# Casts of queries and keys by a two-input VectorE instruction, with the opening of the kernel in another order

## The chip, the cores and the metric

The kernel runs on one core of one Trainium2 chip. The metric is the device time of one execution in microseconds (us); lower is better. A core has five engines that run side by side and wait for each other by semaphores: TensorE (PE, with its weight load PEld), VectorE (DVE), ScalarE (ACT), GpSimd (POOL) and SyncE (SP). Loads and stores are issued from the queues of SP, ACT and POOL.

## The reference

A chunked attention is followed by a two-layer network. Attention has 4 batches, 8 heads, 768 positions and a head dimension of 64. Each chunk of 32 queries sees 8 memory positions, 16 positions to the left, its own 32 and 8 to the right:

```python
k_full = np.concatenate([mem_k, k_ctx], axis=2)
v_full = np.concatenate([mem_v, v_ctx], axis=2)
scores = scale * np.matmul(q_c, k_full.transpose(0, 1, 3, 2))
a = np.exp(scores - np.max(scores, axis=-1, keepdims=True))
out[:, :, c_start:c_end] = np.matmul(a / (a.sum(-1, keepdims=True) + 1e-9), v_full)
```

Its output, as 3072 rows of 512, goes through the network (512 to 2048 and back):

```python
h = x @ w_in
s = np.sin(alpha * h)
g = h + s * s / (alpha + 1e-09)
return g @ w_out
```

Inputs and output are f32; the kernel multiplies in bf16.

## The kernel before, in words

The work is split by batch. Stage i (0 to 3) does the network of batch i, and between its matmuls the attention of batch i + 1. The attention of batch 0 has no network to hide behind: it is the front, stage -1, and the subject here.

The order of everything is written out by hand. `WORDS` has one string of words for each stage, and `Stage.run` issues the instructions of one word after the other. Each engine runs its instructions in that order, and an instruction starts when its engine is free and its inputs and its buffer are there. The words that matter in the front:

- `a<n><engine>` (`do_a`): cast of one tile `kq_f[n]` of two heads, 128x768, from f32 to bf16, into `k_bf` (n = 0 to 2) or `q_bf` (n = 4 to 6), on ACT or DVE. A pair of heads is called a head pair, 0 to 3. These f32 tiles are loaded on the SP queue (k) and the ACT queue (q) before the first word. Head pair 3 is loaded by GpSimd in bf16 at once (`dk068`, `dq068`, L191).
- `k<hp>`, `l<hp>` (`turn`, L312): 12 transposes on TensorE of the keys, or the queries, of a head pair; `K<hp><engine>`, `L<hp><engine>` (`put_k` L323, `put_q` L332): the copy of the result from PSUM into `kT` or `qT`.
- `s<hp><half>` (`u_scores`, L350 and L358): masked scores of one head pair and half of the sequence, and their exponential on ACT (L365). `v<hp><half>` (`u_values`, L377): the product with v, then on DVE the reciprocal of the sums (L386) and the product with it into `x_blk` (L387).
- `T<hp><half>` or `t<hp><half>` (`turned`, L399 and L402): four transposes of `x_blk` and a copy into `xT`, the input of the network, on ACT (T) or DVE (t).
- `V<b><h0><h1>` (`load_v`, L204 to L215): loads of v for heads h0 to h1 of batch b, issued by GpSimd. `I<a><b>` (L249): loads of `w_in`, also by GpSimd. For a batch 0 word like `V024` the heads are 2 and 3.
- `C<x>`: constants. `Cl` transposes alpha (L828) and copies it (L829); `Ck` casts the memory keys (L807), transposes them and puts them into `kT`; `Cm` makes the mask rows; `Cf` and `m0` put the memory values into `vw` (L822, L224); `Cp`, `Cz`, `Cv`, `Cs` are GpSimd's memsets.
- `y<n>` (L725) and `z<n>` (L719): filler matmuls of zeros into a free PSUM bank, 4 of 128 columns for each `y1`, one of 512 columns for each `z1`. Nothing reads their results.
- `We`, `Ws`: loads of ScalarE's table for the exponential or the sine.

PSUM has eight banks; `Banks` hands them out in the order of the words, so an instruction may wait until the earlier user of its bank has been copied out. The network of batch 0 then begins with L457, whose eight matmuls for a block of 128 columns of `w_in` need all of `xT`; its first w_in blocks come with `I02`, the next with `I27`.

Of the kernel before, what the change touches and what calls it, by code (L numbers as in the profile page):

```python
# [17 lines left out]
ALU = mybir.AluOpType  # L18
# [1 line left out]

WORDS = (
    (
# [4 lines left out]
    ),  # L27
    (
# [93 lines left out]
def kernel(  # L122
# [12 lines left out]
    nc = tc.nc  # L135
# [5 lines left out]
    HP = H // 2  # L141
# [175 lines left out]
    def copier(eng):  # L317
        return {"A": nc.scalar.copy, "V": nc.vector.tensor_copy, "P": nc.gpsimd.tensor_copy}[eng]
# [214 lines left out]
    kq = (k_bf, q_bf)  # L533
    todo = [(hp, half) for hp in range(HP) for half in range(2)]

    class Stage:
# [145 lines left out]

        def do_a(self, a):
            hp = int(a[0]) % HP
            dst = kq[int(a[0]) // HP]
            copier(a[1])(  # L686
                dst[:, 2 * hp:2 * hp + 2].rearrange("p h r d -> p h (r d)"), kq_f[int(a[0])][:]
            )

        def do_C(self, a):  # L690
            consts_of[a]()
# [50 lines left out]
    kq_f = [mlp.tile([P, 2, 6 * D], F32, name="kq_f", tag=t) for t in ("u", "s2") * 4]  # L742
# [146 lines left out]
```

## Time and profile before

| | us |
|---|---|
| three runs, median (lowest to highest) | 214.51 (214.29 to 214.54) |
| the profiled execution, its own time | 214.68 |
| span of that execution in the profile | 212.8 |
| TensorE busy in the span | 204.9 (96%) |
| VectorE, ScalarE, GpSimd busy | 139.9, 143.7, 100.9 |

The span runs from the first to the last recorded instruction of the execution; 1.88 us of the profiled time lie outside it. Rows of a timeline give start, length, engine, line, operation, output and input, and in brackets how long the engine was idle before and what released it. Rows of the DMA view give the queue that issued a load, its size and the time from issue to landing. Line numbers are those of the kernel before; in the changed kernel, lines from `do_a` on stand two further down, and ScalarE's casts four.

### The profile page before, as it was taken

Reading aid. Unit: us, or ns where it says so; the run is one execution under the profiler, and the core shown is the slowest. Engines: PE = TensorE matmul, PEld = TensorE weight load, DVE = VectorE, ACT = ScalarE, POOL = GpSimd, SP = SyncE. Lnnn points to the kernel's source line nnn. Section 1 sums busy time; section 2 is a strip of 40 time slices with the busy share of each in tenths; the row PEclk is TensorE's granted clock in tenths of the full one; section 3 lists DMA queues with packets and bytes.
Section 4 is the critical chain, followed back from the end, with each engine's and each line's share of the span. In section 5 each row is a group of like instructions: output and inputs, shape, how many; then the busy total and the mean of one; then the engine's idle time right before and its main releaser. Section 6 shows DMA issues by size and latency. Waiting matters only on the chain.

```text
span 212.8 us, 4568 instructions
## 1 busy us (share of the span) xinstructions
PE 204.9 (96%) x1772; PEld 118.1 (55%) x1772; DVE 139.9 (66%) x210; ACT 143.7 (68%) x229; POOL 100.9 (47%) x142
## 2 busy tenths in 40 slices
PE   7879999999999999999999999999999999999994
PEld 7456665565455556555455555554555555554453
DVE  4788788999452749976766649897247187865010
ACT  2579898978848469968837199887856189891110
POOL 8998605589697297109795048664000022200000
PEclk9999999999999999999999999999999999999999
DMA  5999999999999999999999259999944400000312
GB/s 156 332 158 139 212 207 204 205 139 183 131 160 155 176 114 129 121 144 146 146 152 183 74 125 125 137 157 133 134 104 107 137 0 0 3 2 0 148 52 99
DMA packets 95853, 27.82 MB, mean 131 GB/s; under 512 B 84808, under 2 KB 92376, under 8 KB 95832
## 3 DMA queue, kind: packets, MB, share of 16 engines
q0 software_dynamic: 69152, 13.64, 89.3%
q1 hardware_dynamic: 25720, 12.68, 29.6%
q10 hardware_dynamic: 960, 1.21, 1.7%
q8 instruction: 14, 0.23, 0.6%
q14 instruction: 7, 0.06, 0.1%
HBM read 29.66 MB, written 6.29 MB: 169 GB/s over the span
## 4 chain that ended last, share of the span: by engine, by line
PE 78%; DVE 8%; ACT 5%; DMA 4%; issue 3%; SPq 1%; DVEq 0%; ACTq 0%
PE ps L495 39%; PE ps L457 30%; DMA kq_f<-in_k_dram 4%; PE ps L447 3%; DVE gT L484 2%; PE ps L418 2%; DVE x_blk L387 2%; DVE s L480 2%; ACT s L477 2%; PE ps L399 1%; ACT pt L365 1%; PE ps L312 1%; ACT u L472 1%; DVE q_bf L686 1%; DVE rinv L386 0%
## 5 line engine op out<-in xcount | busy, mean ns | idle before, releaser
L495 PE MATMUL ps<-w_out_sb,gT 128*128 128x512 bf16 (+1 forms) x400 | 89.1, 371 | 0.0
L457 PE MATMUL ps<-xT,w_in_sb 128*128 128x384 bf16 x512 | 85.9, 326 | 0.6 <-DVE gT L484 0.4
L484 DVE SCALAR_TENSOR_TENSOR gT<-s,inv_alpha,ps 128x768 bf16<-128x768 f32 x64 | 63.1, 1012 | 12.3 <-ACT s L477 5.2
L457 PEld LDWEIGHTS <-w_in_sb 128*128 128x128 bf16 x512 | 49.7, 98 | 35.2 <-issue 2.0
L472 ACT ACTIVATE u<-ps,alpha_sb 128x768 f32<-128x768 f32 x64 | 56.6, 894 | 16.9 <-PE ps L457 14.4
L495 PEld LDWEIGHTS <-gT 128*128 128x128 bf16 x400 | 37.1, 98 | 37.1 <-DVE gT L484 0.2
L480 POOL TENSOR_TENSOR s<-u 128x768 f32<-128x768 f32 x11 | 17.2, 1568 | 67.2 <-ACT u L472 56.4
L432 ACT ACTIVATE pt<-ps,biasm 128x256 bf16<-128x256 f32 x72 | 27.1, 488 | 10.5 <-PE ps L418 10.5
L502 DVE COPY o_sb<-ps 128x512 f32<-128x512 f32 (+1 forms) x15 | 10.0, 669 | 27.6 <-PE ps L495 25.7
L480 DVE TENSOR_TENSOR s<-u 128x768 f32<-128x768 f32 x23 | 21.9, 953 | 7.6 <-ACT u L472 7.5
L477 ACT ACTIVATE s<-u 128x768 f32<-128x768 f32 x30 | 25.0, 841 | 0.5
L387 DVE TENSOR_TENSOR x_blk<-ps,rinv 96x512 bf16<-96x512 f32 x32 | 22.0, 687 | 1.1
L502 ACT COPY o_sb<-ps 128x512 f32<-128x512 f32 (+1 forms) x10 | 5.7, 572 | 22.0 <-PE ps L495 22.0
L208 POOL DMA_DIRECT2D vw<-in_v_dram x13 | 12.0, 926 | 6.3 <-PE ps L399 5.4
L386 DVE RECIPROCAL rinv<-ps 96x8 f32<-96x8 f32 x32 | 6.4, 199 | 13.1 <-PE ps L447 12.7
L215 POOL DMA_DIRECT2D vw<-in_v_dram x13 | 13.3, 1024 | 1.6 <-DMA vw<-in_v_dram 1.6
L274 POOL DMA_DIRECT2D kst<-in_k_dram x16 | 13.0, 815 | 1.8 <-DMA vw<-in_v_dram 1.2
L268 POOL DMA_DIRECT2D kst<-in_k_dram x16 | 11.1, 691 | 2.1 <-DMA kst<-in_k_dram 1.0
L281 POOL DMA_DIRECT2D q_bf<-in_q_dram x12 | 10.7, 911 | 0.0
L402 ACT COPY xT<-ps 128x384 bf16<-128x384 bf16 x10 | 5.0, 496 | 8.2 <-PE ps L399 8.2
L447 PEld LDWEIGHTS <-pt 128*128 128x128 bf16 x192 | 8.2, 97 | 4.2 <-ACT pt L432 0.3
L447 PE MATMUL ps<-vw,pt 128*128 128x65 bf16 x192 | 8.9, 193 | 0.0
(83 smaller groups left out, 140.7 us busy)
## 6 DMA issues: line engine op xcount, KB each, us to landing
out_dram<-o_sb SPq DMA_DIRECT2D x23, 256.0 KB, 2.2
q_bf<-in_q_dram POOLq DMA_DIRECT2D x12, 128.0 KB, 7.7
kq_f<-in_k_dram SPq DMA_DIRECT2D x3, 384.0 KB, 6.2
kq_f<-in_q_dram ACTq DMA_DIRECT2D x3, 384.0 KB, 7.9
w_in_sb<-in_moe_w_in_dram POOLq DMA_DIRECT2D x1, 1152.0 KB, 12.9
vw<-in_v_dram POOLq DMA_DIRECT2D x7, 128.0 KB, 7.7
vw<-in_v_dram POOLq DMA_DIRECT2D x8, 112.0 KB, 8.1
kst<-in_k_dram POOLq DMA_DIRECT2D x14, 64.0 KB, 5.5
```

The lines of the kernel that those rows point to most:

```text
L215: nc.gpsimd.dma_start(vw[72:128, c0:hi, 0:D], win(vflat, base + QW * c0 + 48, hi - c0, 56))
L274: nc.gpsimd.dma_start(kst[72:72 + n, j, :].rearrange("p (h d) -> p h d", d=D), k[b, :, QW * j + 48:QW * j + 48 + n, :].rearrange("h p d -> ...
L387: nc.vector.tensor_tensor(out=x_blk[:].rearrange("p g e d -> p e g d"), in0=otv[0:QW, :, :, 0:D], in1=rinv[:].unsqueeze(3).to_broadcast([Q ...
L432: nc.scalar.activation(pt[:, 0:H * QW].rearrange("p (g e c) -> p g e c", g=2, e=4)[:, :, :, 32 * m:32 * m + 32], sc[:, :, 0:4 * QW].rearra ...
L447: nc.tensor.matmul(otv[:, e, hp, :], pt[:, QW * i:QW * i + P], vws[b % 2][:, 2 * hp + e, j, 0:D + 1],)
L457: nc.tensor.matmul(t["hT"][:, hf, 0:HALF], w_in_sb[:, kt, P * t["ft"]:P * t["ft"] + P], t["xT"][:, kt, HALF * hf:HALF * hf + HALF], start= ...
L472: nc.scalar.activation(t["u"][:], t["hT"][:, :, 0:HALF], ACTF.Sin, scale=alpha_sb[:, ft:ft + 1])
L477: nc.scalar.activation(s2[:], u[:], ACTF.Square)
L480: e.tensor_tensor(out=s2[:], in0=u[:], in1=u[:], op=ALU.mult)
L484: nc.vector.scalar_tensor_tensor(out=gT[:, ft, :].rearrange("p (e c) -> p e c", e=2), in0=t["s2"][:], scalar=inv_alpha[:, ft:ft + 1], in1= ...
L495: nc.tensor.matmul(o[:, c0:c1], gT[:, ft, P * s:P * s + P], w_out_sb[:, ft, c0:c1], start=(ft == 0), stop=(ft == FT - 1),)
L502: copier(state["engines"][state["o"] % len(state["engines"])])(o_sb[:, c0:c1], o[:, c0:c1])
```

## The change

VectorE's casts of `kq_f` tiles are no longer copies with a change of type: the same output is written as the larger of the tile and itself, which is the tile, by a two-input instruction. ScalarE's casts stay copies. The string of the front is written in another order. Beside the order it has fewer fillers (`y` 48 matmuls of 128 columns to 16, `z` 14 of 512 columns to 9), two `kT` copies change from ScalarE to VectorE (K1, K3), and three `xT` copies stand on VectorE instead of four. The loads of v's heads 2 and 3 (`V024`) stand ahead of `dk068` and `dq068` on GpSimd's queue, and the cast `a5V` stands ahead of `a2V`. The strings of the other stages are unchanged.

```diff
-        'y1 y1 y1 Ci y1 a4A We y1 Cb a1A y1 y2 y1 y1 dq068 Cl y1 Cm y1 Cf z1 z1 eVA z1 eVA a0A Ck m0 Cz z1 '
-        'dk068 Cp V024 z1 z1 V002 z1 a2V V068 z1 z1 Cv l0 z1 a5V z1 L0A k1 k0 z1 k2 l1 K1A V046 K0A a6V L1A '
-        's00 s10 s11 K2V l2 k3 L2V K3A s01 v11 dm l3 L3A v10 s20 v01 s30 v00 s31 v30 s21 v31 z1 T01 v20 T30 '
-        'I02 Cs T00 v21 t10 T20 t31 z1 t11 I27 t21 Ws '
+        'a4A We Cb Ci eVA a1A y1 Cl V024 Ck Cm Cp Cf z1 m0 z1 y1 z1 Cz dk068 eVA dq068 z1 z1 V002 a5V l0 a2V '
+        'a0A L0A k1 k0 K0A K1V V068 y1 y1 l1 k2 a6V L1A s00 Cv s10 s11 l2 K2V s01 k3 L2V V046 v10 dm K3V l3 '
+        'L3A v11 s30 v00 s31 v01 s20 s21 v30 Cs v31 T10 t01 v20 T00 z1 T11 v21 I02 z1 I27 z1 T31 T30 Ws t20 '
+        'z1 t21 '
...
         def do_a(self, a):
             hp = int(a[0]) % HP
-            dst = kq[int(a[0]) // HP]
-            copier(a[1])(
-                dst[:, 2 * hp:2 * hp + 2].rearrange("p h r d -> p h (r d)"), kq_f[int(a[0])][:]
-            )
+            dst = kq[int(a[0]) // HP][:, 2 * hp:2 * hp + 2].rearrange("p h r d -> p h (r d)")
+            src = kq_f[int(a[0])][:]
+            if a[1] == "V":
+                nc.vector.tensor_tensor(out=dst, in0=src, in1=src, op=ALU.max)
+            else:
+                copier(a[1])(dst, src)
```

## The prediction

> **What bounds the kernel now.** I read the page first, then a table of busy time by stretch, then the chain that ended last.
>
> ```profile
> span 212.8 us, 4568 instructions
> PE 204.9 (96%) x1772; PEld 118.1 (55%) x1772; DVE 139.9 (66%) x210; ACT 143.7 (68%) x229; POOL 100.9 (47%) x142
> 12.30:24.80 12.50, 10.36 (x229) 8.03 (x228) 11.29 (x22) 10.60 (x17) 10.98 (x17) 1.00 2.42 161
> 24.80:186.00 161.20, 160.63 (x1307) 90.07 (x1304) 113.08 (x154) 119.88 (x196) 78.58 (x90) 1.00 1.32 132
> ```
>
> The columns of the two stretches are length, then busy time of PE, PEld, DVE, ACT and POOL. From 24.8 us on TensorE is busy for 160.63 of 161.20 us: there is nothing to win there, and whatever moves the start of that stretch moves the end by as much. The change touches only what comes before, so I ask one question: when does the first matmul with w_in (L457) start?
>
> ```profile
> 2.57 8.45 DMA kq_f<-in_k_dram
> ...
> 11.05 0.56 DVE k_bf L686
> 11.61 1.68 DVE q_bf L686
> ...
> 13.33 0.55 PE ps L312 x12
> ...
> 14.60 2.22 ACT pt L365 x3
> ...
> 24.95 2.62 PE ps L457 x16
> ```
>
> The chain of waits (start, length, what) goes through the last load of k (head pair 2, down at 11.02), then two VectorE casts, then transposes, exponentials and the normalisation. VectorE's own timeline shows the whole stretch:
>
> ```profile
> 5.90 0.17 DVE L829 COPY alpha_sb<-ps 128x16 f32<-128x16 f32 x1 [2.31 <-PE ps L828]
> 9.36 1.22 DVE L224 COPY vw<-memv_st 8x4096 bf16<-8x4096 bf16 x1
> 11.05 0.56 DVE L686 CAST k_bf<-kq_f 128x768 bf16<-128x768 f32 x1 [0.47 <-DMA kq_f<-in_k_dram]
> 11.52 3.15 DVE L686 CAST q_bf<-kq_f 128x768 bf16<-128x768 f32 x2
> 14.60 0.94 DVE L323 COPY kT<-ps 128x768 bf16<-128x768 bf16 x1
> 16.10 0.96 DVE L332 COPY qT<-ps 128x768 bf16<-128x768 bf16 x1 [0.56 <-PE ps L312]
> 17.41 0.20 DVE L386 RECIPROCAL rinv<-ps 96x8 f32<-96x8 f32 x1 [0.35 <-PE ps L377]
> ...
> 23.70 0.69 DVE L387 TENSOR_TENSOR x_blk<-ps,rinv 96x512 bf16<-96x512 f32 x1
> 24.31 1.14 DVE L402 COPY xT<-ps 128x384 bf16<-128x384 bf16 x4
> ```
>
> The eight pairs of reciprocal and x_blk run almost without a gap from 17.41 to 24.39 (23.70 + 0.69), 6.98 us. So the end of the front is VectorE's queue counted from 11.02: casts, two PSUM copies, eight pairs.
>
> **The constants and the filler matmuls.** VectorE stood idle for 2.31 us until 5.90 because the transpose of alpha was queued behind 40 zero matmuls on TensorE. The new order has four of them ahead of it. The constants that follow end at 10.58 now (9.36 + 1.22); 2.31 earlier is 8.3. The order of the constants among themselves changes too, but their instructions are the same, so their sum stays. Their one unknown is when mem_k lands; it was there when its cast ran, and a late landing is in the range. That VectorE is free at 8.3 matters for the next step.
>
> **The casts.** The order is now a5V (q, pair 1), a2V (k, pair 2), a6V (q, pair 2); before, a5V stood behind a2V.
>
> ```profile
> 2.12 0.49 ACTq L748 DMA_DIRECT2D kq_f<-in_q_dram  x1
> kq_f<-in_q_dram ACTq DMA_DIRECT2D x1, 384.0 KB, 7.0
> 39.34 1.03 POOL L215 DMA_DIRECT2D vw<-in_v_dram  x1
> 39.83 0.95 DVE L480 TENSOR_TENSOR s<-u 128x768 f32<-128x768 f32 x1
> ```
>
> q's pair 1 was down at 2.12 + 7.0 = 9.1 and waited for k's pair 2 until 11.02. Moved ahead, its cast fits between 9.1 and 11.02 and leaves the path: 1.68 us gone. The two others become two-input instructions. No row shows a larger-of from f32 to bf16; the nearest is L480, a two-input instruction of one tile with itself, 128x768 f32, 0.95 us, and that one ran beside a load issue on GpSimd (39.34 to 40.37). The bounds are 0.56 (the k cast) and 1.68 (the q cast). I take 0.95. Ends overlap by about 0.09 (11.05 + 0.56 is 11.61, and the next starts at 11.52), so one step of 0.95 costs 0.86.
>
> The q cast was three times as long as the k cast with the same shape; GpSimd issues loads of v all through this time, and in the quoted row the two-input form showed no such stretch. The Trainium skill, SBUF — State Buffer, section "SBUF: two separate sides", says that VectorE and GpSimd share a port pair as an exclusive lock, and that an instruction with two SBUF inputs contends for it only against a GpSimd operation that reads SBUF. By that rule a cast costs 0.95 here even beside load issues, which the 39.83 row agrees with; the sum by it is the one below.
>
> **VectorE's queue after 11.02.** After the change it holds a2V, K1V (a kT copy that ScalarE had), a6V, K2V and L2V: five steps of 0.94 to 0.96, 0.86 each, 4.3 us, so the first reciprocal comes at about 15.4 instead of 17.41. That is 2.0 us. Back goes: K3V, another kT copy taken from ScalarE, +0.86 among the pairs, and one xT copy that now stands ahead of the last pairs (1.14 / 4 = 0.28). Eight pairs at 6.98: 15.4 + 6.98 + 0.86 + 0.28 = 23.5 against 24.39, a gain of 0.9. ScalarE loses two copies and gets one xT copy more; it was busy 10.60 of the 12.50 us, so this costs nothing.
>
> **The loads.** The new order moves the first v load (heads 2 to 3) ahead of q's and k's pair 3 on GpSimd's queue; w_in stays last.
>
> ```profile
> 3.66 0.94 POOL L191 DMA_DIRECT2D q_bf<-in_q_dram  x1
> q_bf<-in_q_dram POOLq DMA_DIRECT2D x1, 192.0 KB, 7.8
> 6.91 0.89 POOL L215 DMA_DIRECT2D vw<-in_v_dram  x1
> 12.03 0.87 POOL L215 DMA_DIRECT2D vw<-in_v_dram  x1
> vw<-in_v_dram POOLq DMA_DIRECT2D x1, 112.0 KB, 7.5
> 17.64 1.51 POOL L249 DMA_DIRECT2D w_in_sb<-in_moe_w_in_dram  x2
> w_in_sb<-in_moe_w_in_dram POOLq DMA_DIRECT2D x1, 640.0 KB, 8.1
> 21.94 0.42 PE L377 MATMUL ps<-vw,pt 128*128 128x65 bf16 x8
> q0 software_dynamic: 54, 0.04, 26.4%
> q0 software_dynamic: 1251, 0.15, 237.1%
> ```
>
> The last two rows (packets, MB, share of the 16 DMA engines) are GpSimd's DMA queue from 8 to 9 us and from 12 to 13: by 9 hardly anything of it had moved although its first load was issued at 3.66, and then it ran full of small packets. So its loads come down some 7.5 to 8 us after issue, in order, and the same bytes are through at the same time in either order. The two pieces of the first v load now take 3.66 to about 5.4, small memsets follow to about 6.3, k's pair 3 is issued then and q's pair 3 at about 7.0, as late as the second v piece before (6.91). It lands at 7.0 + 7.8 = 14.8; its transpose comes at about 15.2 (the queue above, before K3V). Cover 0.4 us. The v load of heads 6 to 7 lands at 12.03 + 7.5 = 19.5 as before. Behind it stand four value products with their pairs: 0.42 for the product, 4 x 6.98 / 8 = 3.5, the xT copy 0.28: 23.7. That is a little later than VectorE's own 23.5, so the loads set the end: 24.39 - 23.7 = 0.7. At the very end fewer VectorE copies of xT are left behind the last pair (two instead of four), worth about 0.1. Sum: **0.8 us earlier**. The larger w_in load is down at 17.64 + 8.1 = 25.7; its first user comes 2.62 us after the first L457, at 24.95 - 0.8 + 2.62 = 26.8, so this gain is covered; it would stop one above 1.8.
>
> The profiled execution took 214.68 (212.8 span and 1.88 around it), so it would take 213.9; it lies 0.17 above the median of the runs shown, 214.51. **Forecast for the median: 213.7.**
>
> **The rivals.**
>
> *The clock of TensorE comes up late (slower).* The row of granted clock says 1.00 throughout, yet matmul rates differ:
>
> ```profile
> 1.20 4.45 PE L725 MATMUL ps<-zeros 128*128 128x128 bf16 x40 [1.20 <-DVE tiny L762]
> 8.29 1.47 PE L719 MATMUL ps<-zeros 128*128 128x512 bf16 x6
> ```
>
> The first 40 filler matmuls take 111 ns per 128 columns, the later ones about 61. The change takes out 32 of the 48 small fillers and five of fourteen large ones, so early TensorE is mostly idle until about 5 us, then gets some 2.7 us of slow filler, then transposes. If full speed comes by 12.4, when the first scores start, nothing is lost: transposes before that wait for loads. From about 13 on it costs. If it came at 16, half of 3.6 us of work is displaced, 1.8 less 0.4 of slack: the last x_blk ends at 23.7 + 1.4 = 25.1 against 24.39, and with the 0.1 of the tail that is 0.6 later: 215.1. For it: TensorE is nearly busy in 12.30 to 24.80 (10.36 of 12.50). Against it: from 10 us on the queue is dense either way. The Trainium skill, TensorE: Matmul & The Clock Gate, Part 1, says that the array runs at half rate until a window of about 3.4 us was busy. By that the fillers from 5 us on should open it by about 12, and the 4.45 us of the first row agrees in size. Chance 0.12.
>
> *q's pair 3 comes too late (slower).* The price is one for one or a little more from 15.2 on, since l3 stands in TensorE's queue ahead of v11 and the rest. At 16.3 the last pair moves by 1.1 to 1.6 from 23.5, to 25.1 at most: 215.1. It decides if the v packets in front delay this load by over a microsecond. For it: cover of 0.4 only. Against: the bytes ahead are the same as those ahead of the second v piece before. Chance 0.08.
>
> *The two-input cast is slow too.* At 1.68 the two on the path cost 2 x 0.73 = 1.5 more: 23.5 + 1.5 = 25.0, 0.6 later than before, 215.1. The 39.83 row speaks against. Chance 0.05.
>
> *The loads eat the gain.* If v or the kq_f loads land 0.5 later, the end is at 24.2 and the gain 0.2 to 0.3: 214.3. The queue is full of packets up to there, so this is the nearest rival. Chance 0.2.
>
> **How the numbers follow.** A measurement of this kernel can tell about 0.2% (0.43 us) from no change. The forecast (chance 0.55) spans 213.0 to 214.0: 213.0 if v lands earlier and VectorE's 0.9 and a shorter wait in the first w_in tiles both count. Loads eating the gain: 0.2, within 0.2%. The three slower cases together 0.25. The range 213.0 to 215.2 takes in the forecast, the loads, and the slower cases up to their worked prices; later ones are left out. Faster 0.55, same 0.2, slower 0.25.
>
> **What would show it.** In the new trace: the cast on q's pair 1 starts near 9.1 and casts take about 0.95 each; the first reciprocal starts near 15.4; the last x_blk ends near 23.7; the first L457 starts near 24.1, and from there TensorE has no new gap. Wrong would be: 111 ns per 128 columns still after 13 us; a wait for q_bf's or vw's DMA above 0.5 us in TensorE's queue; casts above 1.2; or a first L457 that comes early while a later wait for w_in, q_bf or k_bf gives the time back.

## The result, and the profile after

| | before | the change |
|---|---|---|
| median (lowest to highest), 6 runs each, us | 214.52 (214.29 to 215.01) | 216.71 (216.13 to 217.16) |
| ratio, 95% interval | | 1.0095 [1.0073, 1.0117] |
| the profiled execution, its span, us | 214.68, 212.8 | 217.03, 214.9 |

The change makes the kernel slower by about 2.2 us, and the forecast, 213.7 with a range up to 215.2, was wrong in sign. The page of the changed kernel, and its table of busy time by stretch:

```profile
span 214.9 us, 4478 instructions
PE 202.2 (94%) x1716; PEld 116.3 (54%) x1735; DVE 140.1 (65%) x211; ACT 142.6 (66%) x228; POOL 99.5 (46%) x142
12.30:26.60 14.30, 12.71 (x248) 9.90 (x249) 12.52 (x24) 10.26 (x16) 10.95 (x17) 1.00 1.92 142
26.60:188.00 161.40, 159.43 (x1291) 90.11 (x1304) 113.00 (x152) 120.20 (x197) 77.80 (x90) 1.00 1.29 133
```

The stage behind the front is as full as before (159.43 of 161.40 us; some matmul records are missing). What grew is the stretch ahead of it. VectorE's timeline of the changed kernel:

```profile
7.54 1.50 DVE L224 COPY vw<-memv_st 8x4096 bf16<-8x4096 bf16 x1
10.61 0.96 DVE L688 TENSOR_TENSOR q_bf<-kq_f 128x768 bf16<-128x768 f32 x1 [1.57 <-DMA kq_f<-in_q_dram]
12.61 0.96 DVE L688 TENSOR_TENSOR k_bf<-kq_f 128x768 bf16<-128x768 f32 x1 [1.04 <-DMA kq_f<-in_k_dram]
13.49 0.95 DVE L323 COPY kT<-ps 128x768 bf16<-128x768 bf16 x1
14.36 0.95 DVE L688 TENSOR_TENSOR q_bf<-kq_f 128x768 bf16<-128x768 f32 x1
15.22 0.95 DVE L323 COPY kT<-ps 128x768 bf16<-128x768 bf16 x1
16.74 0.96 DVE L332 COPY qT<-ps 128x768 bf16<-128x768 bf16 x1 [0.57 <-PE ps L312]
17.99 0.20 DVE L386 RECIPROCAL rinv<-ps 96x8 f32<-96x8 f32 x1 [0.29 <-PE ps L377]
...
18.83 0.94 DVE L323 COPY kT<-ps 128x768 bf16<-128x768 bf16 x1
...
22.58 0.20 DVE L386 RECIPROCAL rinv<-ps 96x8 f32<-96x8 f32 x1 [0.24 <-PE ps L377]
...
25.65 0.69 DVE L387 TENSOR_TENSOR x_blk<-ps,rinv 96x512 bf16<-96x512 f32 x1
26.42 0.71 DVE L402 COPY xT<-ps 128x384 bf16<-128x384 bf16 x2
```

The casts take 0.96 each, as the prediction had it. But k's pair 2 is cast at 12.61, not at 11.02, and q's pair 1 at 10.61, not at 9.1: both waited for their own loads. The three groups of L457 that open the network, in the kernel before and then in the changed one:

```profile
24.78 17.40 PE L457 MATMUL ps<-xT,w_in_sb 128*128 128x384 bf16 x104
43.86 3.46 PE L457 MATMUL ps<-xT,w_in_sb 128*128 128x384 bf16 x20
```

```profile
26.57 10.86 PE L457 MATMUL ps<-xT,w_in_sb 128*128 128x384 bf16 x64
37.58 6.68 PE L457 MATMUL ps<-xT,w_in_sb 128*128 128x384 bf16 x40
45.94 2.32 PE L457 MATMUL ps<-xT,w_in_sb 128*128 128x384 bf16 x13
```

The last of these groups starts 45.94 - 43.86 = 2.08 us later, nearly all of the 2.1 by which the span grew. It can be taken apart along the prediction's own chain, VectorE's queue (for the end of the front the prediction then took the v loads, 0.2 us later):

| step | before | the change | moved by | forecast |
|---|---|---|---|---|
| first reciprocal | 17.41 | 17.99 | +0.58 | -2.0 |
| from there to the end of the last x_blk | 6.98 | 8.35 | +1.37 | +1.14 |
| from there to the first L457 | 0.39 | 0.23 | -0.16 | -0.1 |
| first L457 to the last group | 19.08 | 19.37 | +0.29 | 0 |

One more wait is new. On GpSimd, first before, then the change, the loads of w_in (L249) and the instruction behind them that waits until one of them is down (L255):

```profile
15.78 0.81 POOL L249 DMA_DIRECT2D w_in_sb<-in_moe_w_in_dram  x1
...
26.05 0.54 POOL L255 DMA_DIRECT2D w_out_sb<-in_moe_w_out_dram  x1 [1.94 <-DMA w_in_sb<-in_moe_w_in_dram]
```

```profile
14.67 0.87 POOL L215 DMA_DIRECT2D vw<-in_v_dram  x1 [2.93 <-DMA vw<-in_v_dram]
...
19.20 2.29 POOL L249 DMA_DIRECT2D w_in_sb<-in_moe_w_in_dram  x3
...
29.32 0.53 POOL L255 DMA_DIRECT2D w_out_sb<-in_moe_w_out_dram  x1 [3.65 <-DMA w_in_sb<-in_moe_w_in_dram]
```

GpSimd waited 2.93 us in the middle of its v loads for an earlier v load to land, which it did not do before; the loads of w_in follow 2.3 us later or more, and the one waited for comes down 3.3 us later (29.32 against 26.05). Counted along GpSimd's queue, the load that waits here is the ninth and the one it waits for is the first; at L255 the 22nd waits for the 14th, which is the larger w_in load (640 KB). In none of the profiles here does GpSimd issue a load earlier than 0.28 us after the load eight places ahead is down. The larger w_in load itself is thus down at 25.77 before (17.64 + 8.12 from issue to landing) and at 29.04 in the change (19.98 + 9.06).

### The profile page after: what moved, and what is told of

The parts are those of the page before. It is cut to its first block, busy times and chain, and to the rows that moved or that the text cites. A ratio compares the mean times of both kernels' runs of the same rounds, so it can differ in the third digit from the quotient of the medians.

```text
span 214.9 us, 4478 instructions
## 1 busy us (share of the span) xinstructions
PE 202.2 (94%) x1716; PEld 116.3 (54%) x1735; DVE 140.1 (65%) x211; ACT 142.6 (66%) x228; POOL 99.5 (46%) x142
## 4 chain that ended last, share of the span: by engine, by line
PE 81%; DVE 6%; DMA 4%; ACT 4%; issue 3%; SPq 1%; DVEq 0%
PE ps L495 38%; PE ps L457 31%; DMA kq_f<-in_k_dram 4%; DVE gT L484 3%; PE ps L447 3%; PE ps L418 2%; PE ps L312 2%; DVE s L480 2%; PE ps L399 2%; ACT s L477 1%; ACT u L472 1%; DVE x_blk L387 1%; PE ps L350 1%; PE ps L377 1%; PE ps L358 1%
## 5 line engine op out<-in xcount | busy, mean ns | idle before, releaser
L495 PE MATMUL ps<-w_out_sb,gT 128*128 128x512 bf16 (+1 forms) x382 | 86.9, 370 | 1.3 <-issue 0.3
L457 PE MATMUL ps<-xT,w_in_sb 128*128 128x384 bf16 x512 | 86.0, 326 | 0.7 <-DVE gT L484 0.4
L457 PEld LDWEIGHTS <-w_in_sb 128*128 128x128 bf16 x512 | 49.7, 98 | 35.4 <-issue 2.1
L502 DVE COPY o_sb<-ps 128x512 f32<-128x512 f32 (+1 forms) x15 | 10.0, 669 | 27.6 <-PE ps L495 25.7
L215 POOL DMA_DIRECT2D vw<-in_v_dram x13 | 12.4, 950 | 4.7 <-DMA vw<-in_v_dram 4.3
L208 POOL DMA_DIRECT2D vw<-in_v_dram x13 | 12.0, 922 | 5.1 <-PE ps L399 4.7
L274 POOL DMA_DIRECT2D kst<-in_k_dram x16 | 12.2, 763 | 1.2 <-DMA vw<-in_v_dram 0.8
L268 POOL DMA_DIRECT2D kst<-in_k_dram x16 | 11.0, 690 | 2.4 <-DMA vw<-in_v_dram 1.2
L281 POOL DMA_DIRECT2D q_bf<-in_q_dram x12 | 10.7, 906 | 0.0
```

The source lines that it names most:

```text
L215: nc.gpsimd.dma_start(vw[72:128, c0:hi, 0:D], win(vflat, base + QW * c0 + 48, hi - c0, 56))
L274: nc.gpsimd.dma_start(kst[72:72 + n, j, :].rearrange("p (h d) -> p h d", d=D), k[b, :, QW * j + 48:QW * j + 48 + n, :].rearrange("h p d -> ...
L457: nc.tensor.matmul(t["hT"][:, hf, 0:HALF], w_in_sb[:, kt, P * t["ft"]:P * t["ft"] + P], t["xT"][:, kt, HALF * hf:HALF * hf + HALF], start= ...
L495: nc.tensor.matmul(o[:, c0:c1], gT[:, ft, P * s:P * s + P], w_out_sb[:, ft, c0:c1], start=(ft == 0), stop=(ft == FT - 1),)
L502: copier(state["engines"][state["o"] % len(state["engines"])])(o_sb[:, c0:c1], o[:, c0:c1])
```

## The experiments

All ratios are to runs of the kernel before on the same chip in the same batch. Single executions of one kernel, the one before too, spread over up to 3 us, so the medians and ratios decide, and one profile shows only one execution. The ratios are not ratios of the medians.

**First: the cast, the order, the v loads, the fillers.** e1_cast is the kernel before with the edit of `do_a` alone:

```diff
+            if a[1] == "V":
+                nc.vector.tensor_tensor(out=dst, in0=src, in1=src, op=ALU.max)
```

> The order of before, with only the three VectorE casts as two-input instructions. Loads theory (the new order of the loads costs the time, the cast itself is harmless): each cast 0.95 us, the two q casts start at 11.9 and 12.8, the first reciprocal about 0.4 to 0.7 earlier than 17.4, time 214.0 to 214.3. Cast theory (the two-input form costs, for instance by holding up GpSimd's load issues): loads of v issued later than before, time 215 or more.

Measured: 214.83, ratio 1.0017 [0.9998, 1.0036]. The two-input cast alone does nothing measurable to the time. Its q casts, which were 3.15 us for two before, are 1.82 for two; k's pair 2 at 10.96 as before:

```profile
10.96 0.96 DVE L688 TENSOR_TENSOR k_bf<-kq_f 128x768 bf16<-128x768 f32 x1 [0.36 <-DMA kq_f<-in_k_dram]
11.83 1.82 DVE L688 TENSOR_TENSOR q_bf<-kq_f 128x768 bf16<-128x768 f32 x2
```

e2_order is its counterpart, the change with `do_a` as it was:

```diff
-                nc.vector.tensor_tensor(out=dst, in0=src, in1=src, op=ALU.max)
+                copier(a[1])(dst, src)
```

> The new order with VectorE's casts still copies. Loads theory: the f32 loads of k and q still land some 1.4 us late (q pair 1 at 10.6, k pair 2 at 12.6), GpSimd still waits near 12, time 216.3 to 217.3. Cast theory: back to 214.7 or less.

Measured: 216.26, ratio 1.0074 [1.0048, 1.01]. So it is the order that costs, not the cast. Its TensorE shows a wait for w_in after 16 matmuls, the only one in any of the profiles:

```profile
25.89 2.77 PE L457 MATMUL ps<-xT,w_in_sb 128*128 128x384 bf16 x16
29.22 14.80 PE L457 MATMUL ps<-xT,w_in_sb 128*128 128x384 bf16 x88 [0.56 <-DMA w_in_sb<-in_moe_w_in_dram]
...
29.45 0.54 POOL L255 DMA_DIRECT2D w_out_sb<-in_moe_w_out_dram  x1 [3.96 <-DMA w_in_sb<-in_moe_w_in_dram]
```

e3_loads is the change with pair 3 loaded ahead of v, as before:

```diff
-        'a4A We Cb Ci eVA a1A y1 Cl V024 Ck Cm Cp Cf z1 m0 z1 y1 z1 Cz dk068 eVA dq068 z1 z1 V002 a5V l0 a2V '
+        'a4A We Cb Ci eVA a1A y1 Cl dq068 Ck Cm Cz dk068 Cp V024 Cf z1 m0 z1 y1 z1 eVA z1 z1 V002 a5V l0 a2V '
```

> The changed kernel with GpSimd's loads in the order of before up to the v load of heads 2 to 3 (q pair 3, k pair 3, then v), nothing else put back. Loads theory: q pair 1 down at 9.1 and k pair 2 at 11.0 again, no wait of GpSimd of 2.9 us near 12, first L457 at 24.0 to 24.8, time 213.7 to 214.5. Clock theory (too few filler matmuls, TensorE slow until 15): loads land as they like, slow transposes until 15 stay and the first L457 comes at 25.4 or later, time 215.2 or more.

Measured: 215.53, ratio 1.0054 [1.0032, 1.0077]. About half of the loss stays. In its profile the first reciprocal is at 15.91, close to the forecast's 15.4, and the first L457 at 24.50; this execution (215.12) was one of its faster ones.

e4_fill puts 32 small fillers back into the change, and e5_both into e3:

```diff
-        'a4A We Cb Ci eVA a1A y1 Cl V024 ...
+        'a4A We Cb Ci eVA a1A y1 y1 y1 y1 y1 Cl y1 y1 y1 y1 V024 ...
```

> The changed kernel with 32 small filler matmuls put back where TensorE was idle before 6 us (16 before the transpose of alpha, 16 after it), so that they delay nothing. Clock theory: transposes of 12 take 0.53 instead of 0.85 from 9 us on, first L457 at 25.7 or earlier instead of 26.6, time 215.8 or less. Loads theory: the transposes get fast too, but k pair 2 still lands at 12.6, the first L457 moves by at most 0.3, time 216.3 or more.

> The changed kernel with the loads of GpSimd in the order of before and the 32 small fillers put back where TensorE was idle. If the fillers matter beside the loads: faster than the kernel with the loads alone put back (215.5), 214.6 or less. If the slow matmuls only fill time in which TensorE waits for k and q: no different from it, 215.2 to 215.8.

Measured: e4 216.64, 1.0092 [1.0059, 1.0124]; e5 215.49, 1.0035 [1.0004, 1.0067]. Neither differs measurably from its kernel without the fillers, so putting them back does not help. By itself that does not rule out TensorE's rate as a cause: in e4's profile twelve transposes take 0.53 us from 7.56 to 11.4 and then 0.84 to 0.85 again from 11.92 to 14, so its TensorE was not at full rate all the way. e9 below is the better test of it.

e6_vfirst puts the v load in front of pair 3 in the order of before (casts as copies), and e7_swap moves q's pair 1 ahead of k's pair 2 in e1:

```diff
-        ... y1 y1 dq068 Cl y1 ... m0 Cz z1 dk068 Cp V024 z1 z1 V002 ...
+        ... y1 y1 V024 Cl y1 ... m0 Cp Cz z1 dk068 dq068 z1 z1 V002 ...
```

```diff
-        'dk068 Cp V024 z1 z1 V002 z1 a2V V068 z1 z1 Cv l0 z1 a5V z1 ...
+        'dk068 Cp V024 z1 z1 V002 z1 a5V V068 z1 z1 Cv l0 z1 a2V z1 ...
```

> The kernel before, casts as copies, with one thing of the change: GpSimd issues the v load of heads 2 to 3 ahead of k's and q's pair 3. Loads theory: q pair 1 lands near 10.4 instead of 9.1, k pair 2 near 12.3 instead of 11.0, GpSimd waits over 2 us for an earlier v load near 12, first sine 1.2 to 1.6 later, time 215.7 to 216.3. Rival (the late loads come from something else in the new front, such as idle TensorE or the earlier constants): k pair 2 near 11.0, time 214.3 to 214.8.

> The order of before with the two-input casts and q pair 1 cast ahead of k pair 2, nothing else. If the casts on VectorE bound the front: the cast of q pair 1 leaves the path after k pair 2 has landed, first sine at 25.4 to 25.7, time 213.7 to 214.2. If the landing of the v loads and ScalarE bound it by now: first sine within 0.2 of the kernel with the casts alone (25.9), 214.4 to 214.9.

Measured: e6 214.95, 1.0001 [0.9975, 1.0028]; e7 214.42, 0.9997 [0.9973, 1.002]. Neither edit costs anything in the order of before, and the swap that the prediction valued at 1.68 us gains nothing that can be measured. But e7 is a poor test of it: VectorE is busy with the constants until 10.6 there, so q's pair 1 is cast from 10.61 to 11.57 and k's pair 2 only at 11.63. In e11 below the constants are early and q's pair 1 is cast at 9.76; the first reciprocal still comes at 16.83, against 16.91 in e1, since VectorE then waits 1.42 us for transposes.

e8_sine delays the first sine by five one-element activations on ScalarE at the end of the front:

```diff
-        'I02 Cs T00 v21 t10 T20 t31 z1 t11 I27 t21 Ws '
+        'I02 Cs T00 v21 t10 T20 t31 z1 t11 I27 t21 Ws Ws Ws Ws Ws Ws '
```

> The kernel before with five more one-element activations on ScalarE between its last copy of xT and the first sine, 1.0 us in all; TensorE's matmuls start as before. If the first sine sets the end of the stretch: the stretch of w_in matmuls ends 0.9 to 1.0 later, time 215.3 to 215.6. If the start of the first w_in matmul sets it, as the prediction had it, 214.3 to 214.7.

Measured: 214.84, 1.0017 [0.999, 1.0044]. The first sine came 0.91 later and the last L457 group 0.56 later in the profile (44.42 against 43.86), but the runs do not tell it from nothing. A delay of half a microsecond there is at the edge of what can be measured.

**Second: which half of the order.** The string is cut at `L0A`. e9_late has the order of before up to there and the change's behind it, e10_early the other way round, and e11_earlyloads is e10 with pair 3 ahead of v. All have the two-input cast. The words that e9 and e10 take from the change:

```diff
+ e9:  L0A k1 k0 K0A K1V y1 y1 l1 k2 ... v30 Cs v31 T10 t01 v20 T00 z1 T11 v21 I02 z1 I27 z1 T31 T30 Ws t20 z1 t21
+ e10: a4A We Cb Ci eVA a1A y1 Cl V024 Ck Cm Cp Cf ... Cz dk068 eVA dq068 z1 z1 V002 a5V l0 a2V a0A V068 Cv
```

> The order of before up to the last cast ahead of L0A (with its 48 small fillers, its order of constants and loads), and from there on the order of the change: K1V, K3V, the new order of scores and values, T10 t01 ... T31 T30 Ws t20 t21. Casts by the two-input instruction, as in the kernel after and in e1. Theory 'opening' (what costs is all ahead of L0A: the loads of v in front, constants and casts earlier, fillers gone): this runs as before and e1 do, ratio 0.998 to 1.002, first L457 at 24.2 to 24.8, first sine 25.8 to 26.4. Theory 'tail' (what e3 still costs, ratio 1.0054, comes from the second half: two more kT copies on VectorE, ScalarE's sine table loaded last): ratio 1.004 to 1.006, and the first sine over 1.5 us behind the first L457.

> The counterpart of e9: the order of the change up to L0A, v's heads 2 and 3 in front of pair 3 included (V068 and Cv stand at the end of that part), and from L0A on the order of before. Two-input casts. Theory 'opening': as slow as the change, ratio 1.008 to 1.010, first L457 26.0 to 26.6, GpSimd waiting 2.5 to 2.9 us with its ninth load, q pair 1 cast at 10.2 or later and k pair 2 at 12.1 or later. Theory 'tail': the loads alone are left, and e6 showed them to cost nothing in the order of before; ratio 1.004 at most. If both halves are needed (the two costs are not a sum), both e9 and e10 are within 0.2% of before.

> As e10, with pair 3 of q and k ahead of v again, as in e3. So it is e3 with the second half of before. Theory 'opening': constants and casts that come earlier and the missing fillers cost what e3 costs: ratio 1.004 to 1.006. Theory 'tail': nothing is left, ratio 0.998 to 1.002, k pair 2 cast at 10.9 to 11.2, first L457 24.0 to 24.6 and first sine 1.5 behind it.

Measured: e9 216.47 (216.16 to 216.60, 4 runs), 1.0097 [1.0072, 1.0123]; e10 214.75 (213.90 to 216.86), 1.0045 [1.0016, 1.0073]; e11 214.35, 0.9996 [0.9978, 1.0014]. The opening alone, early constants, missing fillers and the swapped casts included, costs nothing (e11) and gains nothing; the second half alone costs as much as the whole change (e9). The costs are no sum: with e11's opening in front the second half costs half as much (e3). In e10 the v loads in front cost something on the mean: four of its twelve runs lie at 216.1 to 216.9 and the others at 213.9 to 215.5; why it falls into two groups is open. Its profile is of an execution of the lower group (214.69), and there k's pair 2 is cast at 10.59, earlier than in any other kernel with v in front.

The profiles of e11 and e9, TensorE, then GpSimd (where the string has one line less, as in e11, line numbers are one lower):

```profile
24.33 17.40 PE L456 MATMUL ps<-xT,w_in_sb 128*128 128x384 bf16 x104
...
17.86 1.50 POOL L248 DMA_DIRECT2D w_in_sb<-in_moe_w_in_dram  x2
...
26.04 0.53 POOL L254 DMA_DIRECT2D w_out_sb<-in_moe_w_out_dram  x1 [1.95 <-DMA w_in_sb<-in_moe_w_in_dram]
```

```profile
25.44 10.86 PE L457 MATMUL ps<-xT,w_in_sb 128*128 128x384 bf16 x64
...
18.14 2.29 POOL L249 DMA_DIRECT2D w_in_sb<-in_moe_w_in_dram  x3
...
27.95 0.54 POOL L255 DMA_DIRECT2D w_out_sb<-in_moe_w_out_dram  x1 [3.34 <-DMA w_in_sb<-in_moe_w_in_dram]
```

The first user of the larger load (640 KB, `I27`) stands 16 matmuls, 2.62 us, behind the first L457: at 26.95 in e11 and at 28.06 in e9. The load is down at 25.76 and 27.66, so e11 has 1.2 us to spare and e9 0.4.

e12_table takes another part of the second half by itself, the place of the sine's table in e3:

```diff
-        ... T31 T30 Ws t20 z1 t21 '
+        ... T31 Ws t30 t20 z1 t21 '
```

> e3 with one edit at the end of the front: T31 Ws t30 t20 t21 in place of T31 T30 Ws t20 t21, so that ScalarE loads the sine's table one copy earlier and VectorE takes that copy. Theory 'table' (in e3 the first sine comes 1.72 us behind the first L457, in before 1.50, because the table is loaded last): first sine 0.2 to 0.4 us earlier than in e3 against the first L457, third group of L457 as much, ratio 1.003 to 1.004 where e3 had 1.0054. Theory 'no matter': VectorE's extra copy moves the first L457 later by as much, ratio as e3.

Measured: 215.62, 1.0038 [1.0011, 1.0065]. The distance from the first L457 to the last group went from 19.37 back to 19.09, so that is where the 0.29 of the table above comes from; the time cannot be told from e3's (the medians, 215.62 against 214.32, say 1.0061).

**Third: which part of the second half.** e13_copies is e11 with K1 and K3 on VectorE, e14_scalar is e3 with both back on ScalarE, e15_tail is e3 with everything behind `v30` as in before, and e16_k1 is e11 with K1 alone on VectorE:

```diff
- e13: K1A ... K3A
+ e13: K1V ... K3V
- e14: K1V ... K3V
+ e14: K1A ... K3A
- e15: Cs v31 T10 t01 v20 T00 z1 T11 v21 I02 z1 I27 z1 T31 T30 Ws t20 z1 t21
+ e15: v31 z1 T01 v20 T30 I02 Cs T00 v21 t10 T20 t31 z1 t11 I27 t21 Ws
- e16: K1A
+ e16: K1V
```

> e11 (the opening of the change with pair 3 loaded ahead of v, the second half of before; ratio 0.9996) with one edit: the two kT copies K1 and K3 on VectorE, as the change has them. Theory 'copies' (the second half costs because VectorE, whose pairs of reciprocal and x_blk run without a gap, gets two more copies of 0.95): first reciprocal to first L457 grows from 7.50 to 8.3 or more, or the first reciprocal comes 0.5 to 0.9 later; ratio 1.003 to 1.005. Theory 'order' (it is the order of scores, values, turns and w_in behind it): ratio 0.999 to 1.001.

> The counterpart: e3 (ratio 1.0054, second half of the change) with K1 and K3 back on ScalarE, its order otherwise kept. Theory 'copies': back to before, ratio 0.998 to 1.001, first reciprocal to first L457 7.5 to 7.8. Theory 'order': stays at 1.004 to 1.006, first reciprocal to first L457 8.3 or more.

> e3 with only the last part (from behind v30 on: turns of x, loads of w_in, the sine's table) as in before; K1V, K3V and the order of scores and values stay those of the change. Theory 'turns' (one xT copy of VectorE ahead of the last pairs, and three xT copies of ScalarE and the table behind them, cost): ratio 1.001 to 1.003, first reciprocal to first L457 8.0 to 8.3, first sine 1.5 behind the first L457, third group of L457 0.4 to 0.6 nearer to the first reciprocal than in e3. Theory 'copies': ratio as e3, 1.004 to 1.006.

> A version that might beat both: e11 with K1 alone on VectorE. In e11 VectorE waits 1.42 us for the transposes of q pair 2 behind its last cast, so a copy of 0.95 fits there, and ScalarE, with one copy less, gives the first qT copies earlier. If so: first reciprocal 0.3 to 0.5 earlier than e11's against the landing of k pair 2 (5.0 instead of 5.4 us), ratio 0.996 to 0.999. If ScalarE was not what delayed it: ratio 0.999 to 1.001.

Measured: e13 214.87, 1.002 [0.9995, 1.0045]; e14 215.80, 1.0061 [1.0034, 1.0088]; e15 214.55, 1.0014 [0.9994, 1.0034]; e16 214.76, 1.0021 [0.9998, 1.0045]. The copies are not the cause, in either direction: without them the loss stays (e14), with them it goes (e15). What e15 puts back, the turns of x with the issue of w_in and the sine's table, is. e16 does not beat the kernel before.

**Fourth: what in that part.** e17_win is e3 with the w_in loads issued right behind the last v load and nothing else moved; e18_after_tail is the changed kernel itself with the last part as in before, the same words as in e15:

```diff
- e17: L2V V046 v10 dm K3V ... v21 I02 z1 I27 z1 T31 ...
+ e17: L2V V046 v10 I02 I27 dm K3V ... v21 z1 z1 T31 ...
```

> e3 (ratio 1.0054) with one edit: the two loads of w_in (I02, I27) are issued right behind the last load of v, ahead of dm and of the two memsets Cs, some 1.7 us earlier on GpSimd's queue; the turns, the copies and the sine's table stay those of the change. In e3 a w_in load ended GpSimd's wait at 26.93, and the first user of I27's blocks stands 2.62 behind the first L457, at 27.12: 0.2 us of cover, where before has 1.35 (26.05 and 27.40), and e14 has none (27.42 and 27.38, and its third group of L457 comes 19.83 behind its first, not 19.37). Theory 'w_in' (the second half costs because w_in is issued behind Cs and comes down as the bound): ratio 0.999 to 1.002, w_in's wait on GpSimd ends by 26.2. Theory 'turns' (the order of xT copies and the table on ScalarE costs): ratio 1.004 to 1.006 although w_in comes earlier.

> The changed kernel itself (v ahead of pair 3, K1V, K3V, its scores) with only the last part, from behind v30 on, as in before: what e15 did to e3 (1.0054 to 1.0014), here on the change. If the tail costs here too what it cost there: ratio 1.005 to 1.007 (0.4% less than the change's 1.0095), and what is left is the v loads in front. If the late landing of q and k alone holds the change (first reciprocal at 17.5 to 18.1): ratio 1.008 to 1.010. If the two overlap: 1.001 to 1.004.

Measured: e17 215.30, 1.0019 [0.999, 1.0049]; e18 215.50, 1.0013 [0.9982, 1.0045]. In e18 the v loads are still in front, k's pair 2 is as late as in the change and GpSimd waits 2.78 for a v load, yet most of the 0.95% is gone (the medians say 0.34%, 215.50 against 214.77). VectorE, TensorE and GpSimd of e18:

```profile
12.64 0.96 DVE L687 TENSOR_TENSOR k_bf<-kq_f 128x768 bf16<-128x768 f32 x1 [2.06 <-DMA kq_f<-in_k_dram]
...
17.27 0.20 DVE L385 RECIPROCAL rinv<-ps 96x8 f32<-96x8 f32 x1 [0.21 <-PE ps L376]
...
24.61 0.69 DVE L386 TENSOR_TENSOR x_blk<-ps,rinv 96x512 bf16<-96x512 f32 x1
...
25.69 17.40 PE L456 MATMUL ps<-xT,w_in_sb 128*128 128x384 bf16 x104
44.76 3.46 PE L456 MATMUL ps<-xT,w_in_sb 128*128 128x384 bf16 x20
...
19.84 1.50 POOL L248 DMA_DIRECT2D w_in_sb<-in_moe_w_in_dram  x2
...
27.73 0.53 POOL L254 DMA_DIRECT2D w_out_sb<-in_moe_w_out_dram  x1 [2.22 <-DMA w_in_sb<-in_moe_w_in_dram]
```

The larger w_in load leaves at about the same time in e18 (19.84) as in the change (the second of three from 19.20 on, 19.98), but comes down 1.6 us earlier (27.45 against 29.04; GpSimd's wait ends at 27.73 and 29.32). From issue to landing it took, by the DMA view of e18 and then of the change:

```profile
w_in_sb<-in_moe_w_in_dram POOLq DMA_DIRECT2D x1, 640.0 KB, 7.6
```

```profile
w_in_sb<-in_moe_w_in_dram POOLq DMA_DIRECT2D x1, 640.0 KB, 9.1
```

The larger w_in load in the profile of every kernel, against the ratio; its first user is the first L457 plus 2.62:

| kernel | the load is down | its first user | to spare | ratio |
|---|---|---|---|---|
| e13 | 25.71 | 27.81 | 2.1 | 1.002 |
| e15 | 26.34 | 28.10 | 1.8 | 1.0014 |
| before | 25.77 | 27.40 | 1.6 | 1 |
| e8 | 25.81 | 27.38 | 1.6 | 1.0017 |
| e10 | 25.92 | 27.42 | 1.5 | 1.0045 |
| e17 | 25.99 | 27.46 | 1.5 | 1.0019 |
| e7 | 26.54 | 28.00 | 1.5 | 0.9997 |
| e12 | 26.57 | 27.92 | 1.4 | 1.0038 |
| e6 | 26.07 | 27.34 | 1.3 | 1.0001 |
| e11 | 25.76 | 26.95 | 1.2 | 0.9996 |
| e1 | 26.01 | 27.00 | 1.0 | 1.0017 |
| e5 | 26.88 | 27.84 | 1.0 | 1.0035 |
| e18 | 27.45 | 28.31 | 0.9 | 1.0013 |
| e16 | 25.88 | 26.62 | 0.7 | 1.0021 |
| e3 | 26.65 | 27.12 | 0.5 | 1.0054 |
| e9 | 27.66 | 28.06 | 0.4 | 1.0097 |
| e14 | 27.14 | 27.38 | 0.2 | 1.0061 |
| the change | 29.04 | 29.19 | 0.15 | 1.0095 |
| e4 | 28.75 | 28.79 | 0.0 | 1.0092 |
| e2 | 29.17 | 28.51 | -0.7 | 1.0074 |

Every kernel with 0.5 us or less to spare is slower by 0.54% or more, and every one with more by at most 0.45%. But each row sets one execution against a ratio of many, the line between the two groups was drawn afterwards, and only in e2 does the load come too late. The lowest of the runs point the same way, if less sharply: 216.13 for the change, 216.16 for e9 and 215.65 for e2, then 215.13 for e4, 214.87 for e14 and 214.81 for e3, against 214.65 for e17, 214.19 for e18 and 213.98 for e15. That is what a load would do that sets a floor under the end of the front, while the chain through VectorE varies above it; it is not shown.

How firm this is: that the last part of the order makes most of the loss is shown (e18 against the change, and e15 against e3, whose intervals just touch). That within it the late w_in is what costs rests on e17, whose interval still overlaps e3's, on this table, and on the one wait seen in TensorE (e2, 0.56); in the profiled executions of the change and of e9 TensorE does not wait for w_in. The turns of x and the sine's table cost something too: between the profiles of e18 and the change the last group moves by 1.18 us (44.76 to 45.94), of which the pairs take 0.32 (8.03 to 8.35) and the stretch behind the first L457 0.30 (19.07 to 19.37), less 0.16 between them; the other 0.72 lie ahead of the first reciprocal. And another load of GpSimd's queue fits about as well as w_in: the keys of the next batch. In e14 they are late, and TensorE waits 0.75 us for them:

```profile
44.13 0.53 PE L312 MATMUL ps<-ident,k_bf 128*64 128x128 bf16 x12 [0.75 <-DMA k_bf<-in_k_dram]
```

They are down only 0.04 us ahead of their first transpose in e2 and e9, 0.26 in e12, 0.29 in e4 and 0.41 in the change, against 1.6 before and 0.67 or more in all the others (0.77 in e3, which is slower by 0.54% all the same). No run tells the two loads apart. e9 is not fully explained either: its last L457 group comes 0.95 us later than before, and the span is longer by 1.7.

## Why the prediction was wrong

**"From 24.8 us TensorE is busy ... whatever moves the start moves the end".** Right: 2.08 of 2.1.

**The constants.** Right in direction: the copy of the memory values (9.36 + 1.22) ends at 9.04 in the change (7.54 + 1.50) instead of 10.58, at 8.3 forecast. Most of the difference is VectorE's wait of 1.01 us for mem_k at 5.45, the unknown that the prediction named. It was worth nothing, since VectorE's next work is a load that lands later.

**The casts.** The price was right, 0.96 at 0.95 forecast in every kernel with two-input casts. By the Trainium skill, SBUF — State Buffer, section "SBUF: two separate sides", such an instruction contends with GpSimd only when GpSimd reads SBUF; no two-input cast here took over 0.96, beside GpSimd's load issues too, while copies of the same shape took up to 1.68, so the trace agrees. What the casts save was oversized: e1, e7 and e11 are all within 0.2% of before. The 1.68 us that left VectorE's queue were not all on the path.

**The landing of q and k.** This is the step that failed first, and the largest part of the miss in the profiled execution: the first reciprocal, forecast 2.0 us earlier, came 0.58 later. The prediction took 9.1 and 11.02 over from before, as if they did not depend on what GpSimd's queue carries. In the kernels with v in front k's pair 2 was cast at 12.61 (the change), 12.49, 12.12, 12.64 and 11.70, with one exception at 10.59 (e10); in all others at 10.86 to 11.63. That is 1.6 of the 2.6 us that separate the first reciprocal's -2.0 from its +0.58. "The same bytes are through at the same time in either order" does not even hold for GpSimd's queue. Its first four loads are the same in both kernels; they took 7.7 to 7.8 us before and 9.6 to 10.7 in the change, and the last of them is down at 17.0 (7.27 + 9.7) instead of 14.7 (6.91 + 7.8). The queues of SP and ACT, whose loads came later, were left out. Why the same bytes took longer in this order is not shown. It lay in the rival of the loads, but at 0.5. The rival of q's pair 3 came true in its condition only: that load is the one down at 17.0, past the rival's 16.3, but its transposes start at 17.81 and wait for nothing, since the queue ahead of them was late as well. The late landing took most of the gain away; it does not by itself make the kernel 1% slower than before, as e18 (cast at 12.64, ratio 1.0013) and e6 (at 11.70, 1.0001) show, which have v in front too.

**VectorE's waits, and the clock.** The other 1.0 of those 2.6 lies between the cast of k's pair 2 and the first reciprocal: 17.99 - 12.61 = 5.38 at 4.38 forecast. Without VectorE's two waits for TensorE in that stretch, 0.57 and 0.29 in the rows at 16.74 and 17.99, it would be 4.52, near the forecast. The prediction put these waits at nothing, without a reason, although the rows of before have 0.56 and 0.35 in the same places. In e18, with the same opening and the same landing (12.64), the stretch is 4.63, and only a wait of 0.21 is left. Between these two, TensorE's rate differs. The change first, then e18:

```profile
13.16 0.85 PE L312 MATMUL ps<-ident,q_bf 128*64 128x128 bf16 x12
13.80 0.85 PE L312 MATMUL ps<-ident,k_bf 128*64 128x128 bf16 x12
...
15.51 0.33 PE L358 MATMUL ps<-qT,kT 64*128 64x96 bf16 x8
```

```profile
10.34 0.53 PE L311 MATMUL ps<-ident,k_bf 128*64 128x128 bf16 x12 [1.17 <-ACT k_bf L689]
```

Twelve transposes take 0.85 until after 14 us in the one and 0.53 from 10.3 in the other. So the rival "the clock comes up late" happened in this execution, by TensorE's rate (the granted clock in the profile is 1.00 in both), and cost about 0.7. It is not needed for the verdict: in e9, with the fillers of before, twelve transposes take 0.53 from 8.96 on, and e9 is as slow as the change. The Trainium skill, TensorE: Matmul & The Clock Gate, Part 1, says that the window is free-running and the number of slow matmuls differs from run to run of one kernel. The trace agrees that it varies: two executions with the same opening came to full rate 4 to 5 us apart. Why they lie so far apart no run shows.

**"w_in stays last ... this gain is covered".** This step failed too, and the runs point to the part of the order in which it stands. The prediction took w_in's issue from before (17.64) and checked it against a gain, not against a loss. In the new order `Cs` stands ahead of both loads, the two leave together, and GpSimd's own wait of 2.93 for an earlier v load pushes all of them back: down at 29.04, not at 25.7. Where the prediction had 1.1 us to spare (25.7 against 26.8), 0.15 was left. The wait on GpSimd's queue was in no row of before and in no step of mine. None of the rivals named w_in; a later wait for it stands only among the signs of being wrong. In the profiled execution it cost nothing, since TensorE did not wait; there the 2.08 us are VectorE's chain and the late sine. Over the runs, the last part of the order, which holds the w_in loads, makes most of the loss (e18, e15); whether through w_in, the next batch's keys or the turns of x stays open.

**The pairs and copies.** +1.37 at +1.14 forecast: K3V and the xT copy were priced well, and 0.24 is the wait of VectorE in the row at 22.58, the fifth pair. "ScalarE costs nothing" missed 0.29: the sine's table is loaded behind T30, at 26.89, and the first sine stands 1.72 behind the first L457 instead of 1.50.

## What to carry to other kernels

When an order is rewritten, work out anew when every load is issued, also those that the change only moves past: a load with 1.6 us to spare before (w_in) had 0.15 left after. A queue that waits in the middle delays everything behind it, and a load that then lands last can take away the gains upstream. When engines' steps are added up, put in the waits for other engines that the old timeline shows in the same places. Where one profile differs by less than the runs' spread, halve the change and let medians decide: two runs (e9 and e11) told more than eight that followed single suspicions.

## What the runs showed of the hardware

- In all profiles here GpSimd issues a load only 0.28 us or more after its own load eight places ahead is down, and waits if it must: the ninth for the first, 2.93 us in the change, 2.78 in e18, 1.53 in e6; the 12th for the fourth, 1.10 in e9. In before the ninth did not wait, since the first was down at 11.5 and the ninth's turn came at 12.03. Whether this belongs to the chip or to the program's semaphores no run shows.
- The same 640 KB of w_in took 7.1 to 8.2 us from issue to landing where the 256 KB load left some 1.9 us ahead of it (before, e1, e6, e7, e8, e10, e11, e13, e15, e16, e18), and 8.7 to 9.4 where the two left back to back (the change, e2, e3, e4, e5, e9, e12, e14, e17).
- TensorE reached full rate 4 to 5 us apart in two executions with the same opening (the change and e18), and in e4 fell back from 0.53 to 0.85 us for twelve transposes at about 11.9, 1.7 us after a wait of 2.09 us that ended at 10.18.
